# Chunked attention feeding two dense layer pairs on one core: token blocks of 384 become blocks of 512, with the attention work rearranged around them

## The chip, the cores and the metric

One Trainium2 chip, of which the kernel uses one core. The metric is the device time of one execution in microseconds (us). The kernel before takes 1209.93 us, the median of three runs (1209.13 to 1211.4).

## The reference

Inputs: q, k, v of 4 batches x 8 heads x 768 positions x 64, eight memory keys and values per head, and two pairs of weight matrices of 512 x 2048 and 2048 x 512. All is fp32.

```
for each chunk c of 32 positions:
    keys   = 8 memory keys, then positions 32c-16 .. 32c+39   (64 columns in all)
    scores = q_c @ keys.T / 8 ;  scores -= max ;  a = exp(scores)
    out_c  = (a / (sum(a) + 1e-9)) @ values
x = heads side by side: 3072 tokens x 512
layer pair 1:  h = x @ w_in ;  g = h * clip(h + 3, 0, 6) / 6 ;  x = g @ w_out
layer pair 2:  h = x @ w_in ;  g = max(0.01 h, h)           ;  x = g @ w_out
```

## The kernel before

**The layer pairs.** Each big matrix product is made of three passes over high and low parts (x high times w high, x high times w low, x low times w high), as fp32r matmuls of a 128 x 128 weight tile against one block of tokens as moving columns. Before the change a block has 384 tokens, so there are 8 blocks in each layer pair. In a block the 2048 hidden values are taken in 16 steps of 128 (index f). One step has 12 matmuls for the hidden values (function `hidden`, tile `h`) and 12 that add the step's share to the outputs (function `output`, tiles `ya` and `yb`), so a block has 16 x 24 = 384 big matmuls. Between the two, the hidden tile goes through four operations in a chain: `gate` on ScalarE, `times` on VectorE, `hi` (the rounded copy) on ScalarE, `lo` (the remainder) on GpSimd. The constant `LAG` says how many steps later the output matmuls of a step stand.

**The weights** lie in memory as 8-byte floats. A tile of 128 x 512 is loaded raw (512 KB, `decode`), turned into fp32 by one ScalarE operation (`absolute`) and four VectorE operations (`clamp`, `bits`, `sign`, `low`), and split into high and low parts (`split_w`: a copy and a subtraction). The 32 tiles of layer pair 1 are decoded in the lead and during its first block. The 32 of layer pair 2 are decoded during the later blocks of layer pair 1, parked in memory, and read back when places come free. The pool `w` holds the tiles.

**The attention** is cut into 16 units (function `unit`): half a batch's positions (4 groups of 96 = 384 tokens) times half the heads ("quad"). A unit loads queries and keys (`load_qk`, 4 transfers of 64x2x448 fp32) and values (`load_v`, 12 of 56x2x128 and 4 of 8x6x128), copies the keys into windows on ScalarE or VectorE, then 96 small score matmuls, maximum, subtraction, exponential, sum, normalisation, 6 transposes, a copy, 96 small value matmuls, and the split of the result into `xh` and `xl`, the input of layer pair 1. The first two units go ahead of the first big matmul, and the others are put between big matmuls in the block before their own.

**The order of the work** on every engine is fixed ahead: `schedule` is a planner on the host, which simulates the engines with the costs written beside each task and emits the instructions in the order that it finds. On the chip each engine works through its own list strictly in order and waits by semaphores.

Of the kernel before, what the change touches and what calls it, by code (L numbers as in the profile page):

```python
# [9 lines left out]
F32 = mybir.dt.float32  # L10
# [9 lines left out]
G = 96  # L20
# [14 lines left out]
W_MOST = 122879.9921875  # L35
BLOCKS = [4, 4, 4, 4, 4, 4, 4, 4]
N2 = 384
UNITS_EARLY = 28
LAG = 2

# [159 lines left out]
def tile_attn_moe_moe2(ctx: ExitStack, tc: tile.TileContext, raw, w1i, w1o, w2i, w2o, out):  # L200
    nc = tc.nc
    NMAX = max(max(BLOCKS) * G, N2)

# [7 lines left out]
    KINDS = {  # L211
        "w": (2 * KF + 2, [128, 2, 512], F32R), "wm": (2, [128, 512], F32),
        "raw": (2, [128, NMAX], F32),
        "qk": (2, [128, 2, QK], F32), "kw": (2, [128, 2, 2, NC, W], F32),
        "v": (2, [128, 2, NC, 2 * D], F32), "e": (1, [128, PAIRS, 2, W], F32),
        "mx": (4, [128, 2, PAIRS], F32),
        "xh": (2, [128, KD, NMAX], F32R), "xl": (2, [128, KD, NMAX], F32R),
        "g": (3, [128, 2, NMAX], F32R), "r": (2, [128, NMAX], F32), "ys": (4, [128, NMAX], F32),
    }
# [40 lines left out]
    def dma(nbytes):  # L260
        return nbytes / 330.0
# [17 lines left out]

    blocks = []  # L280
    t0 = 0
    for n in BLOCKS:
        blocks.append((t0, n * G))
        t0 += n * G
    blocks2 = [(t, N2) for t in range(0, NT, N2)]
    items = [("1", j, t, n, f) for j, (t, n) in enumerate(blocks) for f in range(KF)]
# [9 lines left out]

    def decode(src, f, key, early=None, place="wm"):

        t, m = Buf("w"), Buf(place)

# [20 lines left out]

        k = add(load, {"SP": dma(524288)}, key - 30 if early is None else early, allocs=[t])
        k = add(absolute, {"ACT": act(512)}, key, after=[k], allocs=[m], uses=[t])
# [22 lines left out]

    xbuf, xdone = {}, {}

# [8 lines left out]

    def unit(j, quad, key, tag):
        b, half = divmod(j, 2)
        hps, g0 = slice(2 * quad, 2 * quad + 2), 4 * half  # L360

        own = j == 0 and quad == 1
        e = Buf("w" if own else "e")
        qk, kw, v = ([Buf("w" if own else t) for _ in range(2)] for t in ("qk", "kw", "v"))
        p, mx, s = e, Buf("mx"), Buf("mx")
        ps = pt = pv = Buf(tag)
        xh, xl = x_buf("1", j)

# [53 lines left out]
        def greatest(eng):  # L422
# [6 lines left out]
            nc.vector.tensor_reduce(out=mx.t, in_=sv(), op=ALU.max, axis=AX.X)  # L429

        def shifted(eng):
            make(e, ([128, PAIRS, 2, W], F32))
            nc.vector.tensor_tensor(
                out=e.t.rearrange("p c r k -> p r c k"), in0=sv(), in1=mx.t.unsqueeze(3).to_broadcast([128, 2, PAIRS, W]), op=ALU.subtract
            )
# [52 lines left out]
        def lo_x(eng):
            made(xl)
            for i in range(2):  # L490
                minus(eng, x_parts(xl, i), o_parts(i), x_parts(xh, i).bitcast(F32))

        new = [[x] if x.users == 0 else [] for x in (xh, xl)]
        l1 = [add(load_qk(i), {"SP": dma(128 * 2 * QK * 4)}, key - 50, allocs=[qk[i]], issues=3) for i in range(2)]
        l2 = [add(load_v(i), {"ACT": 2600.0} if j == 0 else {"SP": dma(128 * 2 * NC * 512)}, key - 35, allocs=[v[i]], issues=7) for i in range(2)]
        t = [add(windows(i), {"ACT": 1050.0, "DVE": 700.0}, key - 30, after=[l1[i]], allocs=[kw[i]], uses=[qk[i]]) for i in range(2)]
        t = add(scores, {"PE": 2400.0}, key - 16, after=t, allocs=[ps], uses=[*qk, *kw])
        t = add(greatest, {"DVE": 1050.0}, key - 15, after=[t], allocs=[mx], uses=[ps])
        t = add(shifted, {"DVE": 950.0}, key - 15, after=[t], allocs=[e], uses=[ps, mx])
        t = add(exp, {"ACT": act(PAIRS * 128)}, key - 13, after=[t], uses=[e])  # L500
        t = add(total, {"DVE": 1150.0}, key - 12, after=[t], allocs=[s], uses=[e])
        t = add(norm, {"POOL": 1800.0, "DVE": 900.0}, key - 11, after=[t], uses=[e, s])
        t = add(transpose, {"PE": 500.0}, key - 7, after=[t], uses=[e, ps])
        t = add(take_p, {"ACT": act(PAIRS * 128)}, key - 5, after=[t], uses=[pt, e])
        t = add(values, {"PE": 2400.0}, key, after=[t, *l2], uses=[e, *v, ps])
        a1 = add(hi_x, {"ACT": 2 * act(2 * 2 * G)}, key + 1, after=[t] + xdone["1", j][0][:1], allocs=new[0], uses=[pv] + ([] if new[0] else [xh]))
        a2 = add(lo_x, {"DVE": 2 * dve(2 * 2 * G)}, key + 2, after=[a1] + xdone["1", j][1][:1], allocs=new[1], uses=[pv, xh] + ([] if new[1] else [xl]))
        xdone["1", j][0].append(a1)
        xdone["1", j][1].append(a2)

# [112 lines left out]
    def x_again(j, t0, n):  # L623

        xh, xl = x_buf("2", j)
        done = xdone["2", j]
        need = [k for i, (a, m) in enumerate(blocks) if a < t0 + n and t0 < a + m for k in yend["1", i]]
        for k in range(KD):
            key = pos_h["2", j, 0] - BLK + 30 + 12 * k
            r = Buf("raw")  # L630
            t = add(lambda e, r=r, k=k: nc.sync.dma_start(out=make(r)[:, :n], in_=spill[k, :, t0:t0 + n]), {"SP": dma(n * 512)}, key - 10, after=need, allocs=[r])
            t = add(lambda e, r=r, k=k: copy(e, made(xh)[:, k, :n], r.t[:, :n]), {"ACT": act(n), "DVE": dve2(n)}, key, after=[t] + done[0][:1], allocs=[xh] if k == 0 else [], uses=[r] + ([xh] if k else []))
            done[0].append(t)
            t = add(lambda e, r=r, k=k: minus(e, made(xl)[:, k, :n], r.t[:, :n], xh.t[:, k, :n].bitcast(F32)), {"POOL": pool(n), "DVE": dve(n)}, key + 1, after=[t] + done[1][:1], allocs=[xl] if k == 0 else [], uses=[r, xh] + ([xl] if k else []))
            done[1].append(t)


    for j in range(len(BLOCKS)):
        for quad in range(2):
            if j == 0:  # L640
                unit(j, quad, -20.0 * (2 - quad), ("at", "ya")[quad])
            else:
                unit(j, quad, BLK * (j - 1) + (quad + 1) * (BLK - UNITS_EARLY) / 2, "at")
    for f in range(KF):
        for which, src, at in (("1i", w1i, pos_h["1", 0, f]), ("1o", w1o, pos_y["1", 0, f])):
            i = 2 * f + (which == "1o")
            m, k = decode(src, f, at - 8, min(at - 38, -60 + 6 * i))
            split_w(which, f, m, k, at - 7)

    def layer(lay, some):  # L650
# [84 lines left out]
```

## Time and profile before

| | us |
|---|---|
| time, median of 3 runs | 1209.93 |
| the profiled execution's own time | 1211.24 |
| its span, first to last instruction | 1209.5 |
| first big matmul starts | 48.76 |
| 384 big matmuls (one block) done, the first time | 163.57 |
| end of the last big matmul's block | 1204.8 |

Busy shares over the span: TensorE 95%, VectorE 37%, ScalarE 36%, GpSimd 26%. They are averages over stages with different limits, so the stages have to be read one by one. A busy TensorE is not a TensorE at its peak, since the ends of matmuls are modelled: what counts is the distance from the start of one matmul to the start of the next, called the pitch here.

### The profile page before, as it was taken

How to read it: one execution, taken by the hardware profiler on the slowest of the kernel's cores; microseconds unless marked ns; L12 is line 12 of the kernel's file. 1: busy time of each engine (PE TensorE's matmuls, PEld its weight loads, DVE VectorE, ACT ScalarE, POOL GpSimd, SP SyncE). 2: the span in 40 equal slices, each digit the busy share in tenths (PEclk: the TensorE clock that was granted, in tenths of full speed). 3: DMA queues.
4: the chain of work that ended last, by engine and by line, in shares of the span. 5: the costliest groups of instructions: out<-in, count | busy, mean ns of one | idle time of the engine just before them, and what ended most of it. 6: DMA issues, size and time to landing. Idle time of an engine off the chain costs nothing.

```text
span 1209.5 us, 22268 instructions
## 1 busy us (share of the span) xinstructions
PE 1150.1 (95%) x9312; PEld 1127.5 (93%) x9312; DVE 449.6 (37%) x771; ACT 433.7 (36%) x865; POOL 318.8 (26%) x308
## 2 busy tenths in 40 slices
PE   1778799999999999999999999999999999999998
PEld 1657699999999999999999999999999999999998
DVE  1999954454544546443244411111111111111111
ACT  0555543444443444433354423232322223232222
POOL 0221222222232222222322323232323223232222
PEclk9998899999999999999999999999999999999999
DMA  9883113345354443533034301010010101010000
GB/s 230 245 289 104 31 62 84 105 131 139 111 137 124 118 136 110 138 111 80 24 122 127 114 1 53 1 53 1 17 37 14 40 1 53 1 40 1 27 1 27
DMA packets 69349, 97.93 MB, mean 81 GB/s; under 512 B 7808, under 2 KB 52864, under 8 KB 69248
## 3 DMA queue, kind: packets, MB, share of 16 engines
q1 hardware_dynamic: 65776, 94.93, 27.0%
q10 hardware_dynamic: 3472, 1.57, 0.6%
q8 instruction: 73, 1.20, 0.4%
q14 instruction: 28, 0.23, 0.1%
HBM read 75.50 MB, written 20.97 MB: 80 GB/s over the span
## 4 chain that ended last, share of the span: by engine, by line
PE 87%; DVE 5%; DMA 5%; issue 1%; SPq 1%; ACT 1%; ACTq 0%; DVEq 0%
PE h L535 42%; PE ya L587 21%; PE yb L587 21%; DMA w<-in_w1o 2%; PE at L470 2%; DMA w<-in_w1i 2%; DVE wm L316 1%; DVE wm L320 1%; PE at L412 1%; DVE w L277 1%; DMA v<-in_raw 1%; DMA w<-in_raw 1%; DVE wm L312 1%; DVE wm L308 1%; PE at L459 1%
## 5 line engine op out<-in xcount | busy, mean ns | idle before, releaser
L277 POOL TENSOR_TENSOR g<-r,g 128x384 fp32r<-128x384 f32 x256 | 266.2, 1040 | 769.7 <-ACT g L274 741.3
L535 PE MATMUL h<-xh,w 128*128 128x384 f32 x2048 | 404.6, 338 | 12.0 <-ACT w L274 9.9
L587 PE MATMUL ya<-g,w 128*128 128x384 f32 x1536 | 390.5, 338 | 5.4 <-ACT w L274 4.4
L587 PE MATMUL yb<-g,w 128*128 128x384 f32 x1536 | 386.6, 336 | 0.0
L535 PEld LDWEIGHTS h<-xh,w 128*128 128x128 f32 x2048 | 360.3, 189 | 18.0 <-ACT w L274 12.5
L587 PEld LDWEIGHTS ya<-g,w 128*128 128x128 f32 x1536 | 276.0, 189 | 10.1 <-ACT w L274 6.3
L587 PEld LDWEIGHTS yb<-g,w 128*128 128x128 f32 x1536 | 278.6, 189 | 0.0
L557 DVE TENSOR_TENSOR r<-h,r 128x384 f32<-128x384 f32 x128 | 71.3, 557 | 436.6 <-ACT r L551 436.6
L535 PE MATMUL h<-xl,w 128*128 128x384 f32 x1024 | 220.9, 336 | 0.0
L535 PEld LDWEIGHTS h<-xl,w 128*128 128x128 f32 x1024 | 182.5, 189 | 0.2
L274 ACT CAST g<-r 128x384 fp32r<-128x384 f32 x256 | 131.5, 514 | 132.1 <-DVE r L557 74.6
L551 ACT ACTIVATE r<-h 128x384 f32<-128x384 f32 x128 | 62.9, 492 | 274.6 <-PE h L535 274.5
L549 ACT ACTIVATE r<-h,three 128x384 f32<-128x384 f32 x128 | 74.3, 580 | 185.5 <-PE h L535 183.6
L555 DVE SCALAR_TENSOR_TENSOR r<-r,h 128x384 f32<-128x384 f32 x128 | 70.5, 550 | 182.8 <-ACT r L549 182.3
L320 DVE SCALAR_TENSOR_TENSOR wm<-w,wm 128x512 uint32<-128x512 uint32 x64 | 60.1, 939 | 1.1
L277 DVE TENSOR_TENSOR w<-wm,w 128x512 fp32r<-128x512 f32 x64 | 49.4, 775 | 26.1 <-ACT w L274 26.1
L316 DVE SCALAR_TENSOR_TENSOR wm<-w,wm 128x512 uint32<-128x512 uint32 x64 | 53.4, 835 | 1.0
L274 ACT CAST w<-wm 128x512 fp32r<-128x512 f32 x64 | 39.4, 619 | 33.4 <-DVE wm L320 24.1
L305 ACT ACTIVATE wm<-w 128x512 f32<-128x512 f32 x64 | 42.9, 671 | 16.7 <-DVE w L277 16.3
L308 DVE TENSOR_SCALAR wm<-wm 128x512 f32<-128x512 f32 x64 | 35.4, 554 | 35.9 <-ACT wm L305 34.6
L277 POOL TENSOR_TENSOR xl<-raw,xh 128x384 fp32r<-128x384 f32 x32 | 32.1, 1015 | 45.9 <-ACT xh L274 43.1
L455 POOL TENSOR_TENSOR e<-e,mx 128x768 f32<-128x768 f32 x12 | 18.9, 1573 | 63.5 <-DVE mx L451 58.7
(50 smaller groups left out, 354.1 us busy)
## 6 DMA issues: line engine op xcount, KB each, us to landing
qk<-in_raw SPq DMA_DIRECT2D x60, 224.0 KB
v<-in_raw SPq DMA_DIRECT2D x168, 56.0 KB
w<-in_w1i SPq DMA_DIRECT2D x16, 512.0 KB
w<-in_w1o SPq DMA_DIRECT2D x16, 512.0 KB
w<-in_w2i SPq DMA_DIRECT2D x16, 512.0 KB
w<-in_w2o SPq DMA_DIRECT2D x16, 512.0 KB
spill<-ys SPq DMA_DIRECT2D x32, 192.0 KB
raw<-spill SPq DMA_DIRECT2D x32, 192.0 KB
```

What stands on the lines that cost most here:

```text
L274: nc.scalar.copy(out, in_) if e == "ACT" else nc.vector.tensor_copy(out, in_)
L277: engine(e).tensor_tensor(out=out, in0=a, in1=b, op=ALU.subtract)
L305: nc.scalar.activation(out=make(m, ([128, 512], F32)), in_=t.t[:, :, 1].bitcast(F32), func=AF.Abs)
L308: engine(e).tensor_scalar(out=m.t, in0=m.t, scalar1=W_MOST, scalar2=W_LEAST, op0=ALU.min, op1=ALU.max)
L316: nc.vector.scalar_tensor_tensor(out=mu, in0=t.t[:, :, 1], scalar=0xC0000000, in1=mu, op0=ALU.bitwise_and, op1=ALU.bitwise_or)
L320: nc.vector.scalar_tensor_tensor(out=mu, in0=t.t[:, :, 0], scalar=29, in1=mu, op0=ALU.logical_shift_right, op1=ALU.bitwise_or)
L535: nc.tensor.matmul(h.t[:, :n], w.t[:, 1 if p == 1 else 0, k * 128:(k + 1) * 128], x[:, k, :n], start=(p == 0 and k == 0), stop=(p == 2 and ...
L549: nc.scalar.activation(out=make(r)[:, :n], in_=h.t[:, :n], func=AF.Relu, bias=three[:, 0:1], scale=1.0)
L551: nc.scalar.mul(make(r)[:, :n], h.t[:, :n], 0.01)
L555: nc.vector.scalar_tensor_tensor(out=r.t[:, :n], in0=r.t[:, :n], scalar=6.0, in1=h.t[:, :n], op0=ALU.min, op1=ALU.mult)
L557: nc.vector.tensor_tensor(out=r.t[:, :n], in0=h.t[:, :n], in1=r.t[:, :n], op=ALU.max)
L587: nc.tensor.matmul(ys[d // 2].t[:, d % 2, :n], w.t[:, 1 if p == 1 else 0, d * 128:(d + 1) * 128], g.t[:, 1 if p == 2 else 0, :n], start=(f ...
```

## The change

1. Blocks have 512 tokens in both layer pairs, so there are 6 in each. A block still has 384 big matmuls, now of 512 columns.
2. `LAG` goes from 2 to 1.
3. A unit still has 384 tokens, so units and blocks no longer coincide. `to_x` writes a unit's result to the block it belongs to, and the rest goes to the next block, through a stash tile `st` where that one is not open yet. The first block needs four units before it may begin, and these four write their parts directly.
4. The exponential takes 12 instructions of 128x64 straight from the score tile, with the negative maximum as bias and the sum as a second output. The subtraction on VectorE and the sum on VectorE are gone, and a multiplication of the 128x12 maxima is new.
5. Values of the first units are no longer loaded from ScalarE's queue. All loads are on SyncE's queue, interleaved unit by unit with the first weights. The raw load of a weight tile waits for an earlier tile's split.
6. The attention tiles share four places (`a`), except the first three units' tiles, which use places of `w`. The pool `w` has 33 places and not 34, and `g` two and not three.
7. The decoding of layer pair 2's weights starts at 1.25 blocks and not 2.

```diff
-BLOCKS = [4, 4, 4, 4, 4, 4, 4, 4]
-N2 = 384
+N = 512
+NU = 4 * G
-LAG = 2
+LAG = 1
...
-        "w": (2 * KF + 2, [128, 2, 512], F32R), "wm": (2, [128, 512], F32),
...
+        "w": (2 * KF + 1, [128, 2, 512], F32R), "wm": (2, [128, 512], F32),
+        "a": (4, [128, 2, QK], F32), "mx": (4, [128, 2, PAIRS], F32), "st": (2, [128, 2, N // 2], F32),
+        "xh": (2, [128, KD, N], F32R), "xl": (2, [128, KD, N], F32R),
+        "g": (2, [128, 2, N], F32R), "r": (2, [128, N], F32), "ys": (4, [128, N], F32),
...
-        def exp(eng):
-            nc.scalar.activation(out=e.t, in_=e.t, func=AF.Exp, scale=1.0 / 8.0)
+        def exp(gp):
+            def fn(eng):
...
+                for i in range(gp * NC, (gp + 1) * NC):
+                    for r in range(2):
+                        nc.scalar.activation(
+                            out=e.t[:, i, r, :], in_=ps.t[:, r, i * W:(i + 1) * W], func=AF.Exp,
+                            bias=mx.t[:, r, i:i + 1], scale=1.0 / 8.0, accum_out=s.t.rearrange("p r c -> p (r c)")[:, 2 * i + r:2 * i + r + 1],
+                        )
...
-        l2 = [add(load_v(i), {"ACT": 2600.0} if j == 0 else {"SP": dma(128 * 2 * NC * 512)}, key - 35, allocs=[v[i]], issues=7) for i in range(2)]
...
+        l2 = [add(load_v(i), {"SP": dma(128 * 2 * NC * 700)}, key - 38, after=() if own else t, allocs=[v[i]], issues=8) for i in range(2)]
...
-        t = add(norm, {"POOL": 1800.0, "DVE": 900.0}, key - 11, after=[t], uses=[e, s])
+        t = add(norm, {"DVE": 900.0} if direct else {"POOL": 1800.0, "DVE": 900.0}, key - 11, after=[t], uses=[e, s])
...
-    for j in range(len(BLOCKS)):
-        for quad in range(2):
-            if j == 0:
-                unit(j, quad, -20.0 * (2 - quad), ("at", "ya")[quad])
...
+    for u in range(4):
+        unit(u // 2, u % 2, -20.0 * (4 - u), ("at", "ya", "yb", "at")[u], own=u < 3, direct=True)
...
+            before = i - (4 if i >= 2 * KF - 8 else 8)
+            m, k = decode(src, f, at - 8, min(at - 38, -125 + 10 * i), splits[before:before + 1] if before >= 0 else ())
```

**TensorE at the start of the program.** Before, two units stand ahead of the first big matmul (rows of tile `h`); `at` and `ya` are the two units' score tiles in PSUM, 32x64 are score matmuls, 128x128 transposes, 64x32 value matmuls. Of the kernel before:

```order
L412 MATMUL at<-kw,qk 32x64 x48
L412 MATMUL ya<-w 32x64 x48
L459 MATMUL at<-ident,e 128x128 x6
L470 MATMUL at<-e,v 64x32 x48
L459 MATMUL ya<-ident,w 128x128 x6
L470 MATMUL ya<-w 64x32 x48
L412 MATMUL at<-kw,qk 32x64 x48
L535 MATMUL h<-xh,w 128x384 x8
```

Of the change, from the second unit on, with the first row of big matmuls at the end:

```order
L404 MATMUL ya<-w 32x64 x48
L465 MATMUL at<-w 64x32 x48
L454 MATMUL ya<-ident,w 128x128 x6
L404 MATMUL yb<-w 32x64 x48
L465 MATMUL ya<-w 64x32 x48
L454 MATMUL yb<-ident,w 128x128 x6
L404 MATMUL at<-a 32x64 x48
L465 MATMUL yb<-w 64x32 x48
L454 MATMUL at<-ident,a 128x128 x6
L465 MATMUL at<-a 64x32 x48
L578 MATMUL h<-xh,w 128x512 x8
```

All four units have their values multiplied before the first big matmul, where before two had, and a third its scores.

**ScalarE and SyncE at the start.** ScalarE's list of the kernel before, where its queue begins with transfers (`v` and `w` are here the values of units 1 and 2), from the last of them on:

```order
L388 DMA w<-in_raw 56x2x128 x3
L390 DMA w<-in_raw 8x6x128
L305 ACT_TABLE_LOAD
L305 ACTIVATE wm<-w 128x512 x2
L441 ACTIVATE e<-e 128x768
L441 ACTIVATE w<-w 128x768
```

ScalarE's list of the change, from its start, `wm` being a weight tile in decoding:

```order
L270 ACT_TABLE_LOAD
L270 COPY w<-w 128x2x3x56
L270 COPY w<-w 128x2x3x8
...
L296 ACTIVATE wm<-w 128x512
L434 ACTIVATE w,mx<-at,mx 128x64 x6
L270 CAST w<-wm 128x512
L434 ACTIVATE w,mx<-at,mx 128x64 x6
```

The transfers are gone from ScalarE. SyncE's list of the change holds them, `in_raw` being attention input and `in_w1i`, `in_w1o` raw weight tiles:

```order
L369 DMA w<-in_raw 64x2x448 x4
L293 DMA w<-in_w1i 128x1024
L380 DMA w<-in_raw 56x2x128 x3
L382 DMA w<-in_raw 8x6x128
...
L293 DMA w<-in_w1o 128x1024
L369 DMA w<-in_raw 64x2x448 x4
L293 DMA w<-in_w1i 128x1024
```

Each of the first three units is followed there by its values and two weight tiles. Ahead of the fourth unit's queries and keys stand six weight tiles, and ahead of its values eleven.

**TensorE where the first steps of a block stand.** Of the kernel before, three steps of `h` come before the first of `ya` and `yb`:

```order
L535 MATMUL h<-xh,w 128x384 x8
L535 MATMUL h<-xl,w 128x384 x4
L535 MATMUL h<-xh,w 128x384 x8
L535 MATMUL h<-xl,w 128x384 x4
L535 MATMUL h<-xh,w 128x384 x8
L535 MATMUL h<-xl,w 128x384 x4
L587 MATMUL ya<-g,w 128x384 x2
```

Of the change, two:

```order
L578 MATMUL h<-xh,w 128x512 x8
L578 MATMUL h<-xl,w 128x512 x4
L578 MATMUL h<-xh,w 128x512 x8
L578 MATMUL h<-xl,w 128x512 x4
L630 MATMUL ya<-g,w 128x512 x2
```

The output matmuls of a step now stand one step behind its hidden ones and no longer two, and every row has 512 columns.

## Rows read from the trace of the kernel before

**Rows 1.** The page: its head line.

```profile
span 1209.5 us, 22268 instructions
```

**Rows 2.** Windows: stretch, each engine's busy us (x instructions), clock share, DMA share, GB/s.

```profile
0.00:28.00 28.00, 5.31 (x192) 3.72 (x192) 5.06 (x19) 0.03 (x1) 0.74 (x7) 1.00 0.96 225
48.75:163.57 114.82, 93.94 (x884) 82.30 (x883) 108.57 (x194) 60.82 (x113) 24.58 (x20) 0.91 0.46 144
163.57:235.43 71.86, 70.69 (x583) 69.78 (x583) 27.67 (x45) 26.17 (x52) 17.74 (x18) 1.00 0.30 87
235.43:605.62 370.19, 370.19 (x3902) 363.37 (x3902) 173.63 (x284) 149.54 (x313) 97.43 (x91) 1.00 0.41 114
605.62:1138.10 532.48, 532.48 (x3074) 532.48 (x3074) 105.73 (x176) 167.94 (x333) 159.06 (x158) 1.00 0.12 38
```

**Rows 3.** Windows: a stretch of the lead, same columns.

```profile
20.00:40.00 20.00, 3.79 (x88) 3.40 (x92) 9.80 (x17) 6.07 (x8) 3.20 (x2) 1.00 1.04 283
```

**Rows 4.** Timeline of TensorE at the low clock, then windows over that stretch.

```profile
93.23 0.84 PE L587 MATMUL ya<-g,w 128*128 128x384 f32 x2
93.87 0.84 PE L587 MATMUL yb<-g,w 128*128 128x384 f32 x2
...
92.30:95.20 2.90, 2.90 (x11) 2.90 (x10) 2.68 (x6) 1.39 (x3) 0.00 (x0) 0.50 1.08 246
```

**Rows 5.** Timeline of the lead: start, us, engine, operation [idle before, and until what].

```profile
27.97 1.28 ACT L305 ACT_TABLE_LOAD   x1 [27.97 <-DMA w<-in_w1o]
...
34.92 1.54 PE L459 MATMUL at<-ident,e 128*128 128x128 f32 x6 [15.57 <-POOL e L455]
...
37.75 2.90 PE L470 MATMUL at<-e,v 64*64 64x32 f32 x96 [1.29 <-ACT e L274]
...
43.48 1.12 ACT L274 COPY kw<-qk 128x336 f32<-128x336 f32 x4
```

**Rows 6.** Groups by line, VectorE, 48.75 to 163.6: busy us, mean ns | idle before.

```profile
L320 DVE SCALAR_TENSOR_TENSOR wm<-w,wm 128x512 uint32<-128x512 uint32 x28 | 25.2, 899 | 0.2
L316 DVE SCALAR_TENSOR_TENSOR wm<-w,wm 128x512 uint32<-128x512 uint32 x28 | 21.0, 750 | 0.3
L277 DVE TENSOR_TENSOR w<-wm,w 128x512 fp32r<-128x512 f32 x28 | 20.2, 722 | 0.8 <-ACT w L274 0.8
L308 DVE TENSOR_SCALAR wm<-wm 128x512 f32<-128x512 f32 x28 | 14.7, 525 | 0.5 <-ACT wm L305 0.3
L312 DVE TENSOR_SCALAR wm<-wm 128x512 uint32<-128x512 uint32 x28 | 13.4, 480 | 0.4
...
L429 DVE TENSOR_REDUCE mx<-at 128x12 f32<-128x768 f32 x3 | 2.9, 956 | 0.1
```

**Rows 7.** Waits of TensorE, 48.75 to 163.57: total us, times, longest.

```profile
PE h L535 <- ACT w L274: 9.9, 6, 3.7
```

**Rows 8.** Timeline of one step in layer pair 2.

```profile
1010.52 0.85 PE L535 MATMUL h<-xl,w 128*128 128x384 f32 x4
...
1011.47 0.49 ACT L551 ACTIVATE r<-h 128x384 f32<-128x384 f32 x1 [1.05 <-PE h L535]
...
1012.00 0.56 DVE L557 TENSOR_TENSOR r<-h,r 128x384 f32<-128x384 f32 x1 [2.10 <-ACT r L551]
...
1012.59 0.52 ACT L274 CAST g<-r 128x384 fp32r<-128x384 f32 x1 [0.62 <-DVE r L557]
...
1013.18 1.01 POOL L277 TENSOR_TENSOR g<-r,g 128x384 fp32r<-128x384 f32 x1 [1.94 <-ACT g L274]
```

**Rows 9.** Waits of VectorE, 165 to 606: total us, times, longest.

```profile
DVE wm L308 <- ACT wm L305: 24.0, 15, 4.6
```

**Rows 10.** Groups by line and form, whole span: busy us, mean ns | idle before.

```profile
L549 ACT ACTIVATE r<-h,three 128x384 f32<-128x384 f32 x128 | 74.3, 580 | 185.5 <-PE h L535 183.6 <-POOL g L277 1.5
L274 ACT COPY kw<-qk 128x336 f32<-128x336 f32 x48 | 22.6, 471 | 17.2 <-DMA qk<-in_raw 17.1
L274 ACT COPY kw<-qk 128x48 f32<-128x48 f32 x48 | 10.9, 228 | 0.0
```

More of the change, by code (lines that the diff above doesn't have):

```diff
@@ L277, in minus @@
         engine(e).tensor_tensor(out=out, in0=a, in1=b, op=ALU.subtract)
[L280 to L285, printed above, removed]
+    blocks = blocks2 = [(t, N) for t in range(0, NT, N)]
     items = [("1", j, t, n, f) for j, (t, n) in enumerate(blocks) for f in range(KF)]
@@ L295, in tile_attn_moe_moe2, with decode @@
     wbuf, wtask = {}, {}
-    def decode(src, f, key, early=None, place="wm"):
-        t, m = Buf("w"), Buf(place)
+    def decode(src, f, key, early=None, after=()):
+        t, m = Buf("w"), Buf("wm")
         def load(e):
@@ L356, in made, with unit @@
         return b.t if b.t is not None else make(b)
-    def unit(j, quad, key, tag):
+    def unit(j, quad, key, tag, own=False, direct=False):
         b, half = divmod(j, 2)
         hps, g0 = slice(2 * quad, 2 * quad + 2), 4 * half
[L362 to L365, printed above, removed]
+        e = Buf("w" if own else "a")
+        qk, kw, v = ([Buf("w" if own else "a") for _ in range(2)] for _ in range(3))
+        mx, s = Buf("mx"), Buf("mx")
         ps = pt = pv = Buf(tag)
-        xh, xl = x_buf("1", j)
+        jb, at = divmod(j * NU, N)
+        first = min(NU, N - at)
         def of_raw(par, rows, cols):
@@ new lines, in stash @@
+        def stash(eng):
+            make(st)
+            for there, here in parts(st.t, 0, first, NU):
+                copy(eng, there, here)
+        l1 = [add(load_qk(i), {"SP": dma(128 * 2 * QK * 4)}, key - 50, after=() if own else turn, allocs=[qk[i]], issues=3) for i in range(2)]
+        t = [add(windows(i), {"ACT": 1050.0, "DVE": 700.0}, key - 30, after=[l1[i]], allocs=[kw[i]], uses=[qk[i]]) for i in range(2)]
+        l2 = [add(load_v(i), {"SP": dma(128 * 2 * NC * 700)}, key - 38, after=() if own else t, allocs=[v[i]], issues=8) for i in range(2)]
@@ new lines, in unit @@
+        t = add(scores, {"PE": 1300.0}, key - 16, after=t, allocs=[ps], uses=[*qk, *kw])
+        t = add(greatest, {"DVE": 1200.0}, key - 15, after=[t], allocs=[mx], uses=[ps])
+        t = add(exp(0), {"ACT": 6 * 330.0}, key - 13, after=[t], allocs=[e, s], uses=[ps, mx])
+        if not own:
+            turn[:] = [t, *l2]
+        t = add(exp(1), {"ACT": 6 * 330.0}, key - 13, after=[t], uses=[ps, mx, e, s])
+        t = add(total, {"DVE": 350.0}, key - 12, after=[t], uses=[s])
+        t = add(norm, {"DVE": 900.0} if direct else {"POOL": 1800.0, "DVE": 900.0}, key - 11, after=[t], uses=[e, s])
@@ new lines, in unit @@
+        t = add(transpose, {"PE": 600.0}, key - 7, after=[t], uses=[e, ps])
+        t = add(take_p, {"ACT": act(PAIRS * 128)}, key - 5, after=[t], uses=[pt, e])
+        t = add(values, {"PE": 1800.0}, key, after=[t, *l2], uses=[e, *v, ps])
+        to_x(jb, t, key, at, 0, first)
+        if first < NU and direct:
+            to_x(jb + 1, t, key + 1, 0, first, NU)
+        elif first < NU:
+            st = Buf("st")
+            t = add(stash, {"ACT": cost(act, first, NU), "DVE": cost(dve, first, NU)}, key + 1, after=[t], allocs=[st], uses=[pv])
+            to_x(jb + 1, t, pos_h["1", jb + 1, 0] - BLK + 4, 0, first, NU, src=st)
```

114 lines of the change are left out of this document (65 added, 49 removed).

## The prediction

> **What bounds the kernel now.** I read the time by stages first, in the windows [rows 2]. From 605.62 to 1138.10 TensorE is never idle: eight blocks of 384 big matmuls, 3072 (the row's count holds two more that reach over its edges), in 532.48 us. The pitch is 532.48/3072 = 173.33 ns, and a block takes 66.56 us. From 235.43 to 605.62 TensorE is never idle either: five blocks (1920 big matmuls) and ten attention units of 198 small ones. 370.19 - 1920 x 0.17333 = 37.4 us, so a unit costs 3.74 us of TensorE. The next stretch back, 163.57 to 235.43, holds a block, one unit and about 1.5 us of loss. So from 163.57 on the time is a count of matmuls times a pitch. Nothing on another engine matters there as long as it is in time.
>
> Ahead of 163.57 it is different. The first block takes 114.82 us, of which its own matmuls and the unit work inside it need about 76 (66.56 plus 2.6 units). VectorE is busy for 108.57 of the 114.82, and the clock is at 0.91 of full speed [rows 2]. The decoding of a weight tile costs VectorE 899 + 750 + 722 + 525 + 480 ns = 3.38 us [rows 6], and TensorE's longest sum of waits is for such tiles [rows 7]. The first block is therefore VectorE's. And VectorE begins late: ScalarE, which takes the absolute value ahead of each decoding, does nothing until 27.97 us, because its list begins with transfers [rows 5]. The reader should see three stages: a lead up to 48.75, a first block bound by VectorE, and 1046 us bound by TensorE's pitch.
>
> **The change, part by part, first the long stage.** With 512 columns there are 12 blocks of 384 big matmuls in place of 16, 4608 and not 6144. What a matmul of 512 columns costs no row shows. At the low clock (0.50, so 1.2 GHz) four starts of 384 columns lie 0.64 us apart for two [rows 4], that is 320 ns = 384/1.2, with nothing on top. At 2.4 GHz 384 columns would stream in 160 ns, and the pitch is 173.33: 13.33 ns more. If these are a fixed cost of each matmul, 512 columns take 213.33 + 13.33 = 226.67 ns. If the excess grows with the columns, they take 173.33 x 4/3 = 231.1. If it is hidden behind a longer stream, they take 213.3. I take the fixed cost: 13.33 ns are 32 periods of 2.4 GHz, a round number, as belongs to a step done once for each matmul. A cost per column would be one period in every twelve columns, for which nothing in the loop has a reason.
>
> The Trainium skill speaks of this extra: the page "TensorE: Matmul & The Clock Gate", section "Wait — 56ns, not 53.3ns?", gives exactly N/1.2 ns from start to start at the low clock and N/2.4 + about 2.5 ns at the high one, at 128 and at 512 columns alike. The trace agrees at the low clock and with an extra at the high clock only, but has 13.33 and not 2.5. By the page 512 columns would take 215.8 ns, and all blocks behind the first one 46 us less than in my sum.
>
> So a block takes 384 x 0.22667 = 87.04 us, and eleven of them behind the first take 957.4. Sixteen units remain. Four go into the lead, two into the first block, ten behind it: 10 x 3.74 = 37.4. Their matmuls are the same.
>
> **The shorter lag** hides in the same stage. Before, 48 matmuls (8.32 us) lie between the end of a step's hidden values and the first matmul that needs their rounded copy. Now it is 24 x 0.22667 = 5.44 us. In a quiet step the hidden values end at 1010.52 + 4 x 0.173 = 1011.21 and the copy at 1013.11, 1.9 us later, the remainder on GpSimd at 1014.19, 2.98 us later [rows 8]. Extra columns cost ScalarE (471 - 228)/288 = 0.84 ns each [rows 10], so 128 more on three operations add some 0.35 us, and GpSimd's, in proportion, takes 1.35. The copy comes after 2.25 of 5.44 us, the remainder after 3.65 of the 7.25 us that it has. Layer pair 2 has nothing else in the way, so I cost the lag at nothing there. In layer pair 1 other work stands ahead on the in-order lists: VectorE stood up to 4.6 us at a decoding whose absolute value was late, 24.0 us in 15 times [rows 9]. The spare is 3.2 us. A few such waits would now reach TensorE, for a microsecond or so each: I put 3 us (bounds 0 and 15).
>
> **The exponentials** cost ScalarE 12 instructions of 64 columns in place of one of 768. With a bias 384 columns take 580 ns, and 320 columns fewer leave 580 - 269 = 311 ns. Four copies of 471 and 228 ns end after 1.12 us, not 1.40 [rows 5, 10], so about 0.09 us of each is covered by the next: 0.22 to 0.31 each, 2.7 to 3.7 us for a unit. The sum as a second output has no row: I add nothing. Two passes of VectorE over 768 columns (0.956 each [rows 6]) go, for a small multiplication.
>
> **The lead.** Loads come first. Worked out from the shapes, a unit is 0.92 MB of queries and keys and 0.79 MB of values, a raw weight tile 0.52 MB. Ahead of the fourth unit's keys lie three units and six tiles, 9.2 MB with the keys. At 225 GB/s for 28 us and then 283 [rows 2, 3] they land at 28 + (9.2 - 6.3)/0.283 = 38 us, and the fourth unit's values, behind 12.6 MB, at 50. From 38 on the chain of that unit runs: windows 2.2 (two times 1.12), scores (at most the 2.9 of as many value matmuls), maximum 1.2, exponentials 2.7 with about 3 of other ScalarE work between, normalisation 1.4 with about 5 of decoding between on VectorE, transposes 1.5, copy 0.8, values 2.9, the first copy to `xh` 1: 24.6, less if the scores are quicker [rows 5, 6]. That gives a first big matmul at 62 us, for 48.76 now. ScalarE and VectorE have about 40 us of work each in the lead, so neither is later than this chain.
>
> **The first block** then needs 87.04 + 2 x 3.74 = 94.5 us of TensorE: 62 + 94.5 = 156.5 at the earliest. VectorE's bound: before, it needed from the first absolute value (27.97 + 1.3 for a table) to 163.57, 134 us, for 32 tiles, five units and sixteen gates. Now it has the same tiles and gates (each gate 0.13 longer), and six units with two passes fewer each: again about 134. But it can begin near 11 us, once the first keys and the first tile (1.4 MB) have landed. That makes 145 if it never waits, and in the lead it will wait for four units' chains, say 5 to 10 us: 150 to 155. The two bounds lie close together, and where two in-order engines feed each other both lose a little: I take 160 for the end of the first 384 big matmuls (bounds 152 and 176). That is about the 163.57 of before, but with 512 tokens done and six units.
>
> **The sum** for the span: 160 + 957.4 + 37.4 + 3 + the tail. The tail is 1209.5 - 1138.10 - 66.56 = 4.8 now, and 5.1 with longer outputs. Together 1163. The profiled execution took 1.7 us more than its span [rows 1] and 1.3 more than the median of the runs, so the median should be 1163.
>
> **Where the 46 us come from:** 1536 matmuls fewer at 13.33 ns are 20.5. The rest is the start: the time to the end of the first block is the same within 4 us, but a third more tokens and three more units have then been done.
>
> **The rivals.**
> Pitch in proportion: 231.1 ns. Behind the first block 4224 x 4.44 ns = 18.8 more, in it under 2: 1183. For it speaks only that no second size is in the trace. 0.10.
> Pitch with the extra hidden, because 13.33 ns is what the weight load lacks at 384 columns: 213.3 ns, 4224 x 13.33 ns = 56 less, and nothing in the first block, which VectorE then holds: 1107. For it: weight loads are busy all the time [rows 2]. Against it: at the low clock nothing is on top [rows 4], and a transpose with a weight load of the same size takes 1.54/6 = 0.26 us even in the cold lead [rows 5]. 0.09.
> The lead in series: if each of the four units waits for the one before it on ScalarE and VectorE, at 24 us each the first big matmul comes at 8 + 4 x 22 = 96 at worst. Decoding then goes on during the lead, so the block is TensorE's: 96 + 94.5 = 190, in all 1193. Half of that loss is likelier than the whole: 1178. Against it: the first transposes of one unit stand ahead of the next one's scores in the list, so they overlap. 0.12.
> The other side: the sum output makes each exponential dear. At a price p, 48 of them lie on the lead's chain (48 x (p - 0.22)), and behind it 24 batches of six hold ScalarE for 6p against a spare of 3 us. It decides at 48(p - 0.22) + 24(6p - 3) = 46, p = 0.67 us, twice the nearest row. At p = 0.8, near a whole exponential of 768 columns, that is 28 + 43 = 71 more: 1234. 0.03.
>
> **How the numbers follow.** My forecast has 0.66, with a range of its own of 1150 to 1179: first block's end 152 to 170, stalls 0 to 10. The range 1147 to 1187 takes in the proportional pitch and half of the serial lead, and leaves out the hidden extra and the dear exponential: about 0.8. A change of less than 0.2% (2.4 us) cannot be told from none here. Faster by more has 0.96, the same 0.01, slower 0.03.
>
> **What would show it.** Windows in layer pair 2: 87.0 us for a block, 88.7 or 82 by the rivals. First big matmul near 62, 384th done near 160, VectorE over 90% busy between. ScalarE's first work near 7 us. TensorE idle under 5 us in blocks 1 to 5. Exponentials of 0.2 to 0.35 us from start to start. I am wrong if the pitch is not 226.7, if the first block ends beyond 176, or if waits for the hidden values' copies add up.

## The result, and the profile after

The changed kernel takes 1181.24 us, the median of four runs (1180.62 to 1181.96); the kernel before, run beside it, 1210.66 (1209.13 to 1212.77). The ratio is 0.9756, with an interval of 0.9739 to 0.9773. That is inside the range, 18 us above the predicted 1163.

I read the head line and then five windows (columns as in [rows 2]). They answer to the stages of before: the lead's first 28 us and its middle [rows 2, 3], the first block, the blocks of layer pair 1 with units, and six blocks with nothing else. A block's window ends where the 385th big matmul starts, so a wait just ahead of that start lies inside it.

```profile
span 1179.4 us, 19184 instructions
0.00:28.00 28.00, 10.49 (x294) 8.00 (x294) 11.92 (x24) 15.12 (x60) 0.74 (x7) 1.00 0.74 182
20.00:40.00 20.00, 11.17 (x332) 8.83 (x332) 11.15 (x23) 12.39 (x47) 0.00 (x0) 1.00 0.74 183
70.18:175.91 105.73, 98.78 (x782) 79.09 (x780) 95.12 (x161) 63.76 (x165) 25.61 (x19) 1.00 0.50 155
175.91:564.08 388.17, 387.56 (x3516) 318.46 (x3517) 164.31 (x269) 178.48 (x522) 93.57 (x72) 1.00 0.41 114
564.08:1086.32 522.24, 522.24 (x2305) 432.43 (x2304) 106.61 (x140) 152.85 (x257) 151.89 (x118) 1.00 0.12 39
```

From the bottom up: six blocks in 522.24 us are 87.04 a block and 226.67 ns a matmul. Four blocks with ten units took 388.17, so 388.17 - 4 x 87.04 = 40.0 for ten units and all stalls. Behind 175.91 the kernel needs 1179.4 - 175.91 = 1003.5 us, against 42.4 more before (1209.5 - 163.57 = 1045.9). Ahead of it, it is worse: the first 384 big matmuls end at 175.91 for 163.57, 12.3 us later. The difference of the spans, 30.1, is 42.4 - 12.3.

So two places are to be looked into. In the lead the transfers move 182 GB/s at a share of 0.74, where before it was 225 and then 283 GB/s [rows 2, 3]. And the first block lasts 105.7 us, in which TensorE is idle for 7 and VectorE is busy for 95.

The lead first, SyncE's timeline (start, us, what it issues; "x3" is a group of three issues):

```profile
16.79 1.30 SPq L380 DMA_DIRECT2D w<-in_raw  x3
18.13 0.31 SPq L382 DMA_DIRECT2D w<-in_raw  x1
...
26.37 0.31 SPq L382 DMA_DIRECT2D w<-in_raw  x1
26.73 0.35 SPq L293 DMA_DIRECT2D w<-in_w1o  x1
...
43.20 2.55 SPq L369 DMA_DIRECT2D a<-in_raw  x4
```

These are the first and the last of the second unit's sixteen value transfers, and SyncE is at them from 16.79 to 26.7, 9.9 us. Those of the first and third unit take 9.0 and 12.2. Not all of these 31 us is issuing: by SyncE's waits up to 45 us it stands 10.7 of them until an earlier transfer has landed, mostly in the two groups below (total us, times, longest).

```profile
SPq L380 <- DMA w<-in_raw: 4.8, 7, 0.8
SPq L382 <- DMA w<-in_w1i: 4.7, 3, 2.0
```

The fourth unit's queries and keys (the last line of the timeline) stand behind all three and are issued at 43.20, though I had them landed at 38.

Then the first block. First the waits of TensorE in it and in the microsecond behind it (to 176.9), then VectorE's two largest groups, which answer to [rows 6].

```profile
PE ya L630 <- ACT g L270: 3.3, 3, 2.3
PE at L454 <- POOL a L450: 1.5, 1, 1.5
PE ya L630 <- ACT w L270: 1.2, 1, 1.2
PE at L465 <- ACT a L270: 1.0, 1, 1.0
PE ya L630 <- DVE w L273: 0.5, 1, 0.5
```

```profile
L311 DVE SCALAR_TENSOR_TENSOR wm<-w,wm 128x512 uint32<-128x512 uint32 x25 | 21.3, 856 | 0.3
L307 DVE SCALAR_TENSOR_TENSOR wm<-w,wm 128x512 uint32<-128x512 uint32 x25 | 21.1, 846 | 0.4
```

25 tiles are still decoded inside the block. VectorE decoded ten in the lead, so these are 22 of layer pair 1's 32 and three of layer pair 2's. TensorE waits little for tiles now, where before that was its largest wait [rows 7]: 1.2 us at the very end of the window and 0.5 behind it, both for the last ones of layer pair 1. Most of its waiting is for the rounded copy of the hidden values (`g`) and for attention tiles (`at`): 3.3 + 1.5 + 1.0 + 1.2 are the 7 us. The longest wait, on all engines' timeline:

```profile
132.65 0.17 DVE L422 TENSOR_SCALAR mx<-mx 128x12 f32<-128x12 f32 x1
...
132.91 0.32 ACT L434 ACTIVATE a<-at,mx 128x64 f32<-128x64 f32 x1 [0.72 <-DVE mx L422]
133.13 0.19 ACT L434 ACTIVATION_READ_ACCUMULATOR a<-at,mx 128x1 f32 x1
133.22 0.31 ACT L434 ACTIVATE a<-at,mx 128x64 f32<-128x64 f32 x1
...
134.67 0.72 ACT L592 ACTIVATE r<-h,three 128x512 f32<-128x512 f32 x1
...
136.98 0.69 ACT L270 CAST g<-r 128x512 fp32r<-128x512 f32 x1
...
137.72 0.73 PE L630 MATMUL ya<-g,w 128*128 128x512 f32 x2 [2.27 <-ACT g L270]
```

The maxima are ready at 132.8, and only then can ScalarE begin six exponentials. The gate (L592) stands behind these in ScalarE's list and the copy behind six more, so `g` is ready at 137.7. An exponential is two records, the ACTIVATE and the read of its sum, and a pair takes 0.29 to 0.31 us from start to start.

### The profile page after: what moved, and what is told of

Same layout as the page of the kernel before. It is cut to its first block, busy times and chain, and to the rows that moved or that the text cites. A ratio compares the mean times of both kernels' runs of the same rounds, so it can differ in the third digit from the quotient of the medians.

```text
span 1179.4 us, 19184 instructions
## 1 busy us (share of the span) xinstructions
PE 1126.2 (95%) x7776; PEld 925.9 (79%) x7776; DVE 421.1 (36%) x673; ACT 457.4 (39%) x1137; POOL 292.4 (25%) x230
## 4 chain that ended last, share of the span: by engine, by line
PE 85%; DVE 5%; DMA 3%; SPq 2%; ACT 2%; issue 1%; POOLq 0%; POOL 0%; ACTq 0%
PE h L578 41%; PE ya L630 20%; PE yb L630 20%; PE at L465 2%; DMA w<-in_w1i 2%; DVE wm L307 1%; PE at L404 1%; SPq L380 1%; DVE wm L311 1%; DVE w L273 1%; SPq L369 1%; PE at L454 1%; DMA a<-in_raw 1%; DVE wm L299 1%; DMA w<-in_raw 0%
## 5 line engine op out<-in xcount | busy, mean ns | idle before, releaser
L273 POOL TENSOR_TENSOR g<-r,g 128x512 fp32r<-128x512 f32 x192 | 254.5, 1325 | 846.9 <-ACT g L270 846.9
L578 PE MATMUL h<-xh,w 128*128 128x512 f32 x1536 | 384.6, 392 | 0.0
L630 PE MATMUL ya<-g,w 128*128 128x512 f32 x1152 | 354.1, 391 | 5.3 <-ACT g L270 3.3
L630 PE MATMUL yb<-g,w 128*128 128x512 f32 x1152 | 351.2, 389 | 0.0
L578 PEld LDWEIGHTS h<-xh,w 128*128 128x128 f32 x1536 | 288.2, 188 | 60.2
L600 DVE TENSOR_TENSOR r<-h,r 128x512 f32<-128x512 f32 x96 | 66.5, 693 | 439.4 <-ACT r L594 439.4
L578 PE MATMUL h<-xl,w 128*128 128x512 f32 x768 | 206.3, 390 | 0.0
L578 PEld LDWEIGHTS h<-xl,w 128*128 128x128 f32 x768 | 144.2, 188 | 30.1
L270 ACT CAST g<-r 128x512 fp32r<-128x512 f32 x192 | 119.4, 622 | 121.5 <-DVE r L600 67.8
L598 DVE SCALAR_TENSOR_TENSOR r<-r,h 128x512 f32<-128x512 f32 x96 | 65.8, 686 | 147.3 <-ACT r L592 147.3
L592 ACT ACTIVATE r<-h,three 128x512 f32<-128x512 f32 x96 | 66.6, 693 | 130.4 <-PE h L578 129.9
L273 DVE TENSOR_TENSOR w<-wm,w 128x512 fp32r<-128x512 f32 x64 | 56.5, 886 | 20.5 <-ACT w L270 17.6
```

Source lines behind the costliest of these rows:

```text
L270: nc.scalar.copy(out, in_) if e == "ACT" else nc.vector.tensor_copy(out, in_)
L273: engine(e).tensor_tensor(out=out, in0=a, in1=b, op=ALU.subtract)
L578: nc.tensor.matmul(h.t[:, :n], w.t[:, 1 if p == 1 else 0, k * 128:(k + 1) * 128], x[:, k, :n], start=(p == 0 and k == 0), stop=(p == 2 and ...
L592: nc.scalar.activation(out=make(r)[:, :n], in_=h.t[:, :n], func=AF.Relu, bias=three[:, 0:1], scale=1.0)
L598: nc.vector.scalar_tensor_tensor(out=r.t[:, :n], in0=r.t[:, :n], scalar=6.0, in1=h.t[:, :n], op0=ALU.min, op1=ALU.mult)
L600: nc.vector.tensor_tensor(out=r.t[:, :n], in0=h.t[:, :n], in1=r.t[:, :n], op=ALU.max)
```

## The experiments

**Is the lead SyncE's? e1: values in two transfers a unit.** The host lays the values out as `v` wants them; the queue, the order and the bytes that land stay.

```diff
-queue = nc.scalar if eng == "ACT" else nc.sync
-for par in range(2):
...
-        queue.dma_start(out=v[i].t[par * D + NMEM:(par + 1) * D, :, c], in_=rows[:, lo:lo + W - NMEM].rearrange("g r c -> r g c"))
...
+nc.sync.dma_start(out=v[i].t.rearrange("p g c d -> p (g c d)"), in_=vals[b, 2 * quad + i, half])
```

> The changed kernel, with each unit's values laid out by the host in the order of the tile, so that they come by 2 transfers of 128 partitions in place of 16 small ones. Bytes are the same, and the order on every engine is the same. Theory A (SyncE's queue): in the lead of the changed kernel SyncE needs 9 to 12 us to issue the 16 transfers of one unit's values, the fourth unit's keys are issued at 43.2 us, and the DMA engines are busy for only 0.75. Without that the fourth unit's keys land about 10 us sooner: first big matmul at 60 to 63 us in place of 70.2, VectorE starved less, 384 big matmuls done at 162 to 170 in place of 175.9, time 1167 to 1175 for 1181. Theory B (the units' own chain on ScalarE, with the read of the sum behind each exponential, sets the lead): first big matmul at 68 or later, time 1178 to 1181.

Measured: 1172.07 us, ratio 0.9683 (0.9669 to 0.9698). Windows of its lead and first block, then SyncE's timeline:

```profile
20.00:30.00 10.00, 3.60 (x181) 3.35 (x165) 8.60 (x19) 8.48 (x38) 0.00 (x0) 0.73 1.05 288
60.80:166.61 105.81, 98.86 (x784) 78.98 (x780) 95.44 (x161) 63.82 (x166) 25.66 (x19) 0.98 0.46 149
```

```profile
10.37 1.30 SPq L375 DMA_DIRECT2D w<-in_v  x2
...
24.47 2.60 SPq L369 DMA_DIRECT2D a<-in_raw  x3
```

Two issues take 1.3 us, the fourth unit's keys are issued from 24.47 and not 43.20, the rate is 288 GB/s at a share of 1.05, and the first big matmul starts at 60.80 for 70.18. The lead was the queue's. e1 also makes the pieces longer: a value tile now has, by its shape, 3 KB in a row for each partition, where a transfer of 56x2x128 had pieces of 512 bytes. No run parts the two. Most of the gain is that the transfers' engines are kept busy: at a share of 1.05 the old pieces, which moved 182 GB/s at 0.74, would have come to about 258 (an estimate). The block, however, has the same length and the same busy time of VectorE: the late start is not why it is long.

**Is a second queue better? e2: the first three units' values on ScalarE's queue**, as before the change.

```diff
-l2 = [add(load_v(i), {"SP": dma(128 * 2 * NC * 700)}, key - 38, after=() if own else t, allocs=[v[i]], issues=8) for i in range(2)]
+l2 = [add(load_v(i), {"ACT": 2600.0} if own else {"SP": dma(128 * 2 * NC * 700)}, key - 38, after=() if own else t, allocs=[v[i]], issues=8) for i in range(2)]
```

> The changed kernel, with the values of the first three units issued from ScalarE's queue as in the kernel before. Theory A: SyncE gets through its list 20 us sooner, but ScalarE's first work waits for its own issues as in the kernel before (27.97 us there), and by then 38 us of ScalarE's lead work are left: first big matmul at 66 to 76 us, time 1176 to 1190. Theory B: ScalarE is the lead's chain, so its late start moves everything: first big matmul beyond 85, time over 1192.

Measured: 1206.54 us, ratio 0.9969 (0.9957 to 0.9981). That is the time of theory B, but its reason did not come: the first big matmul starts at 70.04, as theory A said, and not beyond 85. ScalarE's first work in the change and in e2, then e2's windows of the lead's first 28 us, of the lead and of the first block, and TensorE's largest wait in that block:

```profile
5.32 1.28 ACT L270 ACT_TABLE_LOAD   x1 [5.32 <-DMA w<-in_raw]
25.32 1.28 ACT L434 ACT_TABLE_LOAD   x1 [25.32 <-DMA w<-in_raw]
```

```profile
0.00:28.00 28.00, 5.32 (x192) 3.72 (x192) 5.49 (x22) 2.66 (x11) 0.74 (x7) 1.00 0.83 201
0.00:70.04 70.04, 24.72 (x793) 21.00 (x793) 31.96 (x91) 26.06 (x117) 0.74 (x7) 0.92 0.80 193
70.04:206.77 136.73, 111.31 (x1077) 86.87 (x1075) 119.86 (x205) 79.33 (x228) 25.96 (x19) 0.93 0.50 150
```

```profile
PE ya L630 <- ACT w L270: 13.8, 4, 6.7
```

ScalarE works from 25.32 and no longer from 5.32, so VectorE gets 32.0 us of work done in the lead and not 41.2. In the block it has 119.9 where the change has 95.1, and TensorE waits for its tiles; the block lasts 31 us longer. Not all of that is lost: the planner found another order, with about one and a half units more in this block (1077 small and big matmuls for 782) and so fewer behind it, and the span is 25.1 us longer (1204.5). The first big matmul comes no earlier (70.04). With ScalarE's list taken up by transfers all but 4 us of the change's gain are gone. The Trainium skill says on the page "DMA: Bandwidth & Descriptors", section "Issuing engines are not separate DMA queues", that issuing from several engines saves only the sequencer's issue time, usually small beside the transfer. e1 and e2 agree with the first half: the second queue brought the first 28 us from 182 to 201 GB/s, fewer issues on one queue brought 288 (20 to 30 us). The second half does not hold for 16 small transfers a unit, at which SyncE was for 9 to 12 us, about a third of it waiting.

**Is the first block VectorE's? e4: a shorter decoding.** The last decoding operation handles 8 of 512 columns; 504 columns of each tile lack their lowest bits.

```diff
-nc.vector.scalar_tensor_tensor(out=mu, in0=t.t[:, :, 0], scalar=29, in1=mu, op0=ALU.logical_shift_right, op1=ALU.bitwise_or)
+nc.vector.scalar_tensor_tensor(out=mu[:, :8], in0=t.t[:, :8, 0], scalar=29, in1=mu[:, :8], op0=ALU.logical_shift_right, op1=ALU.bitwise_or)
```

> The changed kernel with the last of the four decoding operations of a weight tile on 8 of its 512 columns (the lowest three bits of the other weights stay zero, so this step is left out for them). VectorE loses about 0.57 to 0.77 us for each of the 32 tiles of layer pair 1, some 24 of them after the first big matmul. If VectorE holds the first block, the 384th big matmul is done 8 to 14 us sooner (162 to 168) and the time is 1167 to 1174. If the shorter lag or TensorE itself holds it, it moves by under 4 us: 1177 to 1181.

Measured: 1171.67 us, ratio 0.968 (0.9664 to 0.9696). Window of the first block:

```profile
69.88:167.42 97.54, 97.27 (x782) 79.65 (x781) 82.79 (x159) 64.11 (x165) 25.56 (x19) 1.00 0.56 171
```

With 12 us of VectorE's work gone from the block, it ends 8.5 us sooner, and TensorE is idle for 0.3 and not 7.0. The exponentials still come in batches of six. So the waits for `g` and for attention tiles were waits for operations that stood behind decoding on VectorE.

**Both: e8 = e1 + e4** (with e4's columns left out).

> The values in two transfers and the last decoding operation on 8 of 512 columns together. If the lead is SyncE's and the first block VectorE's, the two gains add up: first big matmul at 60 to 62, first block 97 to 99 us, time 1161 to 1165. If they are the same gain seen twice: 1168 to 1172.

Measured: 1164.12 us, ratio 0.9607 (0.9591 to 0.9623). Window of the first block:

```profile
62.24:159.46 97.22, 96.90 (x785) 79.03 (x781) 82.36 (x160) 63.83 (x165) 25.35 (x19) 0.98 0.50 162
```

The gains nearly add: 9.2 and 9.6 us alone, 17.1 together. With both holdups away the kernel has the very terms of my sum, 62.2 for 62, 159.5 for 160, and 1164 for 1163. That does not make the sum right: it had the whole decoding in it, and e8 leaves out 12 us of it in the block.

**A whole kernel with less in the block: e9 = e1, with layer pair 2's decoding from 1.75 blocks on.**

```diff
-through_dram("2i", w2i, f, 1.25 * BLK + 24 * f, pos_h["2", 0, f] - 40)
+through_dram("2i", w2i, f, 1.75 * BLK + 24 * f, pos_h["2", 0, f] - 40)
```

> The values in two transfers, and the decoding of layer pair 2's weights begins at 1.75 blocks and not at 1.25. In the changed kernel three tiles of layer pair 2 are loaded before the last of layer pair 1, and VectorE decodes them at 3.4 us each. If they stand in the way of the last tiles, the first block takes 95 to 99 us for 105.8 and the time is 1161 to 1166. If they only fill VectorE's idle time, the time is 1169 to 1173. Should the decoding come too late for layer pair 2, TensorE would idle beyond the sixth block.

Measured: 1170.56 us, ratio 0.9658 (0.9644 to 0.9673); e1's interval (0.9669 to 0.9698) overlaps it. Window of the first block, and its largest wait:

```profile
62.24:165.95 103.71, 98.55 (x784) 80.04 (x781) 88.85 (x149) 62.13 (x162) 25.94 (x19) 0.97 0.41 130
```

```profile
PE ya L623 <- ACT g L270: 2.7, 2, 2.5
```

VectorE has 6.6 us less to do than in e1, and the block is 2.1 us shorter: the wait for the last tile at its end (1.0 us in e1) is gone, the longest, of 2.5 us, stays. Those tiles mostly filled VectorE's idle time. By its median this is the fastest kernel here that computes everything, but not clear of e1.

**What is the block size worth? e5: N = 384 with all else of the change; e6: the same with LAG = 2 and three places of `g`.**

```diff
-N = 512
+N = 384
...
-LAG = 1
+LAG = 2
...
-"g": (2, [128, 2, N], F32R),
+"g": (3, [128, 2, N], F32R),
```

> The changed kernel with blocks of 384 tokens; lag, places, exponentials and the order of loads are those of the change. If the pitch is 173.33 ns again and VectorE holds the first block whatever its size, the first block ends near 163 as before, and behind it stand 15 blocks of 66.56 us and twelve units of about 3.8 (1044 us), 1210 to 1216 in all: then the size of the blocks is the whole gain. Rival: the new start is a gain by itself, and the time is 1185 to 1200.

> As the run with blocks of 384, with a lag of 2 steps and three places for the split hidden values, as in the kernel before. If the shorter lag costs TensorE only a few waits of VectorE's and ScalarE's lists, the two are within 5 us of one another; if it is a steady cost, this one is faster by over 8 us.

Measured: e5 1222.9 us, ratio 1.0088 (1.0073 to 1.0104); e6 1222.86, ratio 1.0089 (1.006 to 1.0118). TensorE's largest wait in e5's first block, then windows of that block and of a late one:

```profile
PE h L578 <- ACT w L270: 19.0, 8, 12.5
```

```profile
40.64:170.98 130.34, 95.21 (x980) 83.52 (x979) 109.49 (x200) 74.21 (x207) 23.05 (x17) 0.88 0.55 171
947.50:1014.06 66.56, 66.56 (x386) 66.56 (x385) 10.00 (x18) 18.65 (x39) 20.12 (x20) 1.00 0.08 24
```

Without the larger block the rest of the change is slower than before: its first block waits for decoded tiles. e5 was 7 us beyond what I gave it, and its rival (1185 to 1200) is out. Against the change: behind the first block e5 has 15 x 66.56 - 11 x 87.04 = 41.0 us more of big matmuls. Half of that, 1536 x 13.33 ns = 20.5, is the fixed cost, and half, 128 tokens x 384/2.4 ns = 20.5, is tokens that the change has done by the end of its first block. That block ends 4.9 us sooner in e5, and stalls, units and tail make up 3.5: 41.0 + 3.5 - 4.9 = 39.6, the difference of the spans (1219.0 and 1179.4). At 384 tokens the lag, together with the third place of `g`, is worth nothing in the total (e6); no run has 512 tokens with a lag of 2.

**A third size for the pitch: e7, N = 256, one run** (the stash keeps 256 columns, and only two units write directly, as a smaller block needs).

```diff
-N = 512
+N = 256
```

> Blocks of 256 tokens, for the pitch alone (the third and fourth unit go through the stash, since their columns belong to later blocks). A fixed 13.33 ns for each matmul gives 256/2.4 + 13.33 = 120.0 ns in layer pair 2, an extra in proportion to the columns 115.6, an extra that depends on something else neither. The time is not the point; with 24 blocks of 384 x 120 = 46.1 us and VectorE's first block it should lie at 1240 to 1290.

Measured: 1289.71 us, one run. Window of a late block:

```profile
1190.02:1236.10 46.08, 46.08 (x387) 46.08 (x386) 7.55 (x18) 13.93 (x36) 13.26 (x18) 1.00 0.05 15
```

46.08/384 = 120.0 ns = 256/2.4 + 13.33. Three sizes now lie on N/2.4 + 13.33 ns, with nothing left over.

**The exponentials. e3: the sum back on VectorE; e10: also the subtraction, and one exponential of 768 columns.**

```diff
-bias=mx.t[:, r, i:i + 1], scale=1.0 / 8.0, accum_out=s.t.rearrange("p r c -> p (r c)")[:, 2 * i + r:2 * i + r + 1],
+bias=mx.t[:, r, i:i + 1], scale=1.0 / 8.0,
...
+nc.vector.tensor_reduce(out=sf, in_=ev(), op=ALU.add, axis=AX.X)
```

```diff
-for i in range(gp * NC, (gp + 1) * NC):
-    for r in range(2):
-        nc.scalar.activation(
...
+nc.vector.tensor_tensor(
+    out=e.t.rearrange("p c r k -> p r c k"), in0=sv(), in1=mx.t.unsqueeze(3).to_broadcast([128, 2, PAIRS, W]), op=ALU.subtract
+)
...
+nc.scalar.activation(out=e.t, in_=e.t, func=AF.Exp, scale=1.0 / 8.0)
...
+nc.vector.tensor_reduce(out=sf, in_=ev(), op=ALU.add, axis=AX.X)
```

> The changed kernel without the sum output of the exponentials: VectorE sums the 768 columns (0.95 us) as in the kernel before. Shows the price of the sum: exponentials 0.22 us from start to start if the read of the sum costs ScalarE the rest of the 0.29 now. Theory A: the lead is SyncE's, so the first big matmul stays at 68 to 72 and the time within 4 us of 1181. Theory B: 48 reads of some 0.08 us leave ScalarE's chain and 4 sums of 0.95 us enter VectorE's: 3 to 5 us sooner in the lead and 1174 to 1179.

> The changed kernel with the exponentials of the kernel before: subtraction on VectorE, one exponential of 768 columns, sum on VectorE (the planner counts the sum at 0.7 us). ScalarE loses 2.7 us for a unit and VectorE gains 1.75. If the first block is held by VectorE alone, it grows by some 3 to 6 us and the time is 1183 to 1188. If the batches of six on ScalarE, which hold up the gate and the rounded copy, are what makes TensorE wait there, the block gets shorter by up to 4 us and the time is 1174 to 1180.

Measured: e3 1184.45 us, ratio 0.9784 (0.977 to 0.9799); e10 1198.43, ratio 0.9908 (0.9892 to 0.9925). A row of e3, twelve exponentials in a group with the operation after it; then, of e10, the first block's window and TensorE's longest wait:

```profile
12.00 2.56 ACT L434 ACTIVATE w<-at,mx 128x64 f32<-128x64 f32 x12 [2.16 <-DVE mx L422]
14.36 0.70 ACT L270 CAST w<-wm 128x512 fp32r<-128x512 f32 x1
```

```profile
72.00:189.05 117.05, 101.01 (x878) 81.08 (x876) 104.21 (x168) 60.30 (x121) 28.09 (x21) 0.95 0.50 150
```

```profile
PE ya L627 <- ACT w L270: 8.9, 1, 8.9
```

An exponential alone takes (14.36 - 12.00)/12 = 0.20 us, so the read of its sum adds 0.09, 1.1 us a unit on ScalarE, for 0.95 on VectorE. e3's first expectation came (first big matmul at 71.73, time within 4 us). Its loss of 3 us would fit that VectorE's microsecond is the dearer one here, but does not show it: its interval and the change's still overlap (0.977 against 0.9773), and the planner puts half a unit more into its first block (879 matmuls for 782).

In e10 VectorE has 104.2 us to do in the block, and the window is 11.3 us longer. Of the window 8.9 us are one wait at its very end, for the last tile of layer pair 1 (1.2 in the change), and 1.2 us are scores of half a unit more. Without these the block is 2.4 us longer, a little under the 3 to 6 that I gave to VectorE. The late tile was in no expectation of mine; it is the largest part of the 17 us that e10 lost for 2 to 7. e10's rival, that the exponentials hold up the first block by coming in batches, can be worth little: the waits for `g` fall only from 3.3 us to 2.3 without the batches, and in e4, which keeps them, there are none.

## Why the prediction was right, and where it was off

The measured 1181.24 us lie inside the range, 1147 to 1187, but outside the forecast's own, 1150 to 1179. The room above 1179 was left for a pitch in proportion and for half of a serial lead. Neither of them is what happened, so that the range held is in part luck. The first block's end, 175.91, stays inside its bounds by 0.1 us.

**The pitch** was right: 226.67 ns, with a fixed 13.33 at three sizes (e7, e5, the change). Both pitch rivals are out. So are the 215.8 ns that I estimated from the Trainium skill's page "TensorE: Matmul & The Clock Gate", section "Wait — 56ns, not 53.3ns?", which gives N/2.4 + about 2.5 ns at the high clock. From the first block's end to the end of the span I had 957.4 + 37.4 + 3 + 5.1 = 1002.9 us, and it took 1003.5.

**The lag** at nothing in layer pair 2 was right. The 3 us that I put for it in layer pair 1 were not what filled that term: behind the first block TensorE waits 0.5 us for a tile and 0.3 for a remainder and never for the copy, while the ten units took 39.4 us of TensorE for the 37.4 that I had. Two errors of about 2 us cancel. In the first block, where VectorE is late, the waits for the copy come to 3.3 us; before, with two steps of lag, there were none.

**The step that failed is "160 for the end of the first 384 big matmuls"**: 175.9, of whose 15.9 us the lead has 8.2 and the block 7.7. The remaining 2 us to 1181 are 0.6 in the other terms, and a median that lies beside the profiled execution and not 1.3 below it.

In the lead I worked with bytes "at 225 GB/s for 28 us and then 283". The 225 were of two queues that issue side by side, and the 283 of a stretch in which ScalarE's transfers were soon through and SyncE's were few and large. With all on one, SyncE's 9 to 12 us for a unit's values set the rate, 182 GB/s. e1 shows it: with the same bytes in fewer issues the first big matmul comes at 60.8, as predicted. My series rival had its size (half of it was 15 us) but not its cause. It names 24 us for a unit and adds up 22. And what I set against it reads the other way: transposes that stand ahead of the next unit's scores on an in-order list hold those up. In the lead TensorE stood 4.3 to 7.5 us at each of the four groups of transposes. e1, which keeps that order, shows that the forecast's lead had room for it.

In the block I took the later of two bounds, TensorE's 156.5 and VectorE's 150 to 155, and some. VectorE's was worked out from the start of the kernel, as if its work could flow evenly over lead and block. But VectorE is busy for only 41 us of the lead, and what is left, 95 us, is as long as TensorE's own 94.5. I had both numbers, 134 us in all and about 40 in the lead, and did not take one from the other. Two in-order engines with nearly equal work in one stage wait for each other here: the block takes 11.2 us more than the 94.5. TensorE is idle for 7.0 of them. Its first twelve big matmuls also take 2.1 us more than at the pitch. The rest, some 2 us, I do not assign; in e4 and e8, where the waits are gone, 0.8 are left of it, and the first big matmuls are still slow.

**The exponentials** at 0.22 to 0.31 us came out at 0.29, but by two errors: alone one takes 0.20, and "I add nothing" for the sum's output was wrong, since it is an instruction of its own, worth 0.09. The dear exponential, my rival for the slower side, needed 0.67. That they relieve VectorE, which I counted only as two passes fewer, is worth more than I thought: e10 loses 17 us, some 8 of them at one late tile. The planner also finds another order there, so the 17 are not VectorE's passes alone.

**Where the gain comes from** was right in kind: 20.5 us of fixed cost and 20.5 of tokens done in the stage that VectorE holds (e5). Of these 41.0 the change loses about 12 again, since its first block ends at 175.91 and not, as before, at 163.57.

## What to carry to other kernels

A fixed cost per matmul is found by comparing one size at two clocks or two sizes at one; here it then priced two further block sizes to the hundredth of a nanosecond. Price a move of transfers to one queue by the number of issues as well as by bytes: a rate seen with two queues is not that of one. In a stage where two engines that feed each other have about the same work, neither bound holds: add their mutual waits, or relieve the one whose work can be done outside the stage.

## What the runs showed of the hardware

The first ten or so big matmuls after the units' 32-column ones are slow though the granted clock reads 1.00. TensorE's timeline of the change in three views, then that stretch's window, and the same stretch's window of e1:

```profile
70.18 3.78 PE L578 MATMUL h<-xh,w 128*128 128x512 f32 x8
71.20 2.76 PE L578 MATMUL h<-xh,w 128*128 128x512 f32 x6
73.33 0.63 PE L578 MATMUL h<-xh,w 128*128 128x512 f32 x1
```

```profile
70.18:73.76 3.58, 3.58 (x11) 2.81 (x10) 2.87 (x9) 1.66 (x5) 0.00 (x0) 1.00 1.06 268
60.80:64.38 3.58, 3.58 (x13) 2.77 (x9) 3.07 (x9) 1.61 (x6) 0.00 (x0) 0.50 0.61 150
```

The third of the eight starts at 71.20 and the eighth at 73.33: five distances of 426 ns, which is what 512 columns take at 1.2 GHz (427), with nothing on top, as 384 columns had [rows 4]. In e1, where the clock reads 0.50 from 30 us on, the eight take the same 3.58 us. So here the clock in the windows does not tell the two levels apart, and the distance of starts does.
